# A sliding-window attention and MoE kernel: fewer f32 loads at the start, masks built earlier, and a new hand-written order

## The chip, the core and the metric

The kernel runs on one core of a Trainium2 chip. A core has five engines with queues of their own: TensorE (PE, matrix products into PSUM; its weight loads are the row PEld), VectorE (DVE), ScalarE (ACT), GpSimd (POOL) and SyncE (SP). SP, ACT and POOL also issue DMAs, which sixteen DMA engines carry out. The metric is the device time of one launch in microseconds (us), the median of several runs; lower is better.

## The reference

Two stages. Attention over 8 batches, 8 heads, 576 positions and head size 64; heads 0 to 3 look back over 32 neighbours (plain heads), heads 4 to 7 over 32 positions at a stride of 4 (dilated heads). Its output, 4608 rows of 512, goes through a two-layer network with a SiLU between.

```python
mask_plain = (rel >= 0) & (rel < window)                                   # window = 32
mask_dil = (rel >= 0) & (rel < window * dilation) & (rel % dilation == 0)  # dilation = 4
scores = np.where(masks, scale * q @ k.T, -1e9)
attn = softmax(scores) @ v
...
x = attn_out.transpose(0, 2, 1, 3).reshape(B * S, H * D)   # 4608 x 512
h = x @ w_in                                               # 512 -> 2048
g = h * (1.0 / (1.0 + np.exp(-h)))
return g @ w_out                                           # 2048 -> 512
```

## The kernel before

All work is in f16 with f32 sums. The attention is computed batch by batch, the network in ten groups of tokens: groups 0 and 1 have 256 tokens each, all of batch 0, groups 2 to 9 have 512. A group needs the attention output of the batches that its tokens lie in, so attention of later batches is mixed with the network of earlier tokens.

**Steps and the table.** Every piece of work is a step with a short name, and the long string TABLE (lines 11 to 117) lists the steps in the order in which they are put into the engines' queues. Nothing reorders them afterwards: each engine takes its own instructions in the table's order and waits where data is not there. A name's first token emits its PE part into the PSUM buffers named behind the equals sign (a, b, x, y, u, z, or s for a pair); each later token emits the next part on another engine (A is ACT, D is DVE; S and A behind an output step name the queue that issues its store). The names that matter below:

- `0N0` and so on: early casts and clears of batch 0, without PE work.
- `bTA..`, `bTD..`, `bTS..`, `0TR`: transposes on PE that turn loaded q and k of batches 0, 1 and 2 (`b`) so that the head dimension lies on partitions; TD is for dilated heads.
- `bS0` to `bS6`: scores and their exponential; `bP..` and `bD..`: attention times v for plain and dilated heads; `bXP..`, `bXD..`: transposes of the result into the network's input `xA`.
- `lg.f`: layer 1 of group g, columns f (four matmuls); for groups 8 and 9 `lg.j.i` is one of seven smaller products of a Strassen scheme. `yg.t.n`: layer 2, for groups 2 to 9 again seven products. `u`, `a`, `t`, `w`, `v`: sums for these schemes, on DVE.
- `z..`: a filler matmul on nothing.

**Loads.** The input is f32. Nearly all loads are issued by POOL and cast to f16 on the way (`issue_part`, `issue_vraw`, `issue_vp_first`, then the list ORDER). They come back to back: batch 0, then w_in in the pieces w0b, w0a, w1, w2, w3, then batch 1 (d1, p1), w_out mixed with batch 1's v, then batch 2 (`0B`). Three loads at the very start are uncast and issued by SP: the dilated heads of k and q of batch 0 (`issue_raw`, line 282, 384 KB each, into memory that later holds `kqT`), which the steps 0N0 to 0N3 cast on ACT and DVE, and the head of v (line 336, 96 KB, into `xA`), which 0N12 casts into `vp`.

**Batches 3 to 7** take another way: POOL casts q and k into DRAM (`issue_cast`, line 286, tensor kq_s), and SP reads them back with transposing DMAs (`issue_turn`, lines 300 and 303, steps `bT`, four each: k and q of plain heads into `nat`, k and q of dilated heads into `kqT`). The POOL step `bL` (`loads_gen`) waits for an earlier batch's `kqT` with two tiny copies (line 477), loads v, and issues the cast. For batches 5 to 7 the result goes to DRAM (`bW0` to `bW3`, line 708) and comes back transposed into `xA` (`bX0`, `bX1`, line 469), all on SP. The steps `f0` to `f10` (`hold`, line 1055) are tiny POOL copies that read a finished layer-1 column, so that what stands behind them in POOL's queue comes no earlier; `f2` reads column 3 of group 6, the output of `l6.3`.

**The start in code order.** SP's three loads, clears, eight warm-up matmuls (line 340), the clear of the identity on DVE, POOL's first load (k), the identity on POOL (line 344), POOL's other loads, a clear of `vraws[1]` on ACT (line 351), more clears on DVE, and then the masks (lines 364 to 371), which need the identity.

Of the kernel before, what the change touches and what calls it, by code (L numbers as in the profile page):

```python
# [23 lines left out]
l1.9=t 1TS0=D 1TS0=A 1TS1=a 1TS1=D 1S6=s l1.11=t y0.0.0=y 1TS1=D l1.9 1S6 1S3 0B l1.11 l1.10=t 1S6 l1.8=a
1S4=s 1TA1k=z 1S4 1S4 l1.10 1V1=A 1S5=bx 1S5 y0.1.0=u 1TA1k=D 1S4 1S5 l1.8=t 1S2=s 1S2 1S2 1S0=xz 1V0=D 1D03=b
1D03 1D03 1S0 l1.8 y0.1.1 y0.0.1 1S0 1S6 1S1=s 1S1 1S5 1D10=a 1D02=x 1D02 1D02 1D10 1S0 1D11=z 1D12=b 1D10
y0.0.2 l1.14=x l1.14=s y0.1.2 1D12 1D01=a 1D12 1S2 1D13=b y0.1.3 y0.1.3=A 1D11 1D01 y0.0.3 1S1 1D13 y0.0.3=A
y1.0.0=x 1D01 w1 1D11 1S1 1D00=y 1P3=z 1P0=u 1D13 1P3 1P1=b 1P1 1P3 1P4=a y1.0.1 1D00 l1.13=z l1.13=t 1P4 1D00
1P0 1P0 1XD0=y 1XD0=A 1P1 y1.0.2 1XD0=A l1.13 1P4 1P2=u 1XP3=b 1XP1=y 1XP1=D y1.0.3 y1.0.3=A 1P2 1P2 1XP0=a
2TA1k=z 1XP3=D 1XP4=u 1XP2=y 1XD1=b 1XP4=A 2TD3=x 2TD1=u 1XP0=D 1XP2=A 2TD3=D 1P5=a 1P5 2V0=A 1XD1=A 1XD1=A  # L30
2TD1=A l2.1=y l2.0=x y0.1.3=A 1P5 l2.1=s l2.0=t 2TA1k=D 2TD0=u 2TD2=z y1.1.0=y 2TD0=A 2TD2=D 2S5=s 2S4=ub 2S4
2S4 w1 2S6=za y1.1.1 2S5 y1.1.2 y1.1.3 2S6 2S5 2V1=A w1 l2.0 2S3=s 2S6 w0 y1.1.3=A v1 2TS0=a 2TS0=A 2TA1q=b
2TA1q=A 2TA0q=x 2TS1=z 2TA0k=y 2TA0k=A 2TA0q=D 2TS1=D 2S3 l2.2=u 2TS0=D 2S1=xb l2.2=t 2TS1=D 2S0=ya 2S1 2S3
2S0 2S2=s 2S2 l2.3=z l2.3=t l2.4=x 2S3 2S0 2S1 l2.2 l2.8=u l2.8=s 2S0 l2.6=y l2.4=s l2.6=s 2S4 l2.5=a l2.5=s
l2.3 2S6 2D03=b 2D03 2D03 l2.7=z 2S1 2P1=u 2P1 l2.10=b 2D01=y l2.7=s 2P1 l2.10=s 2D00=u 2D01 2S5 2XP1=x 2XP1=A
l2.9=a 2D01 2D00 2D00 2D12=b 2D10=y 2D12 l2.11=x 2P0=z l2.9=s 2D10 2D10 2D13=a 2D11=u l2.11=s l2.14=y 2D12 2P0
2D13 2D13 2P2=b 2D02=a l2.13=x 2D11 2P0 2P2 2D11 l2.12=u l2.14=s l2.13=s 2D02 2D02 0B 3T 3T 3T 3T 3L 2P2
2XD0=y 2S2 2S2 y1.1.3=A l2.12=s w0 2XP0=z 2P3=a l2.15=x 2XP0=A 3L 2XD0=A 2P3 2P3 y0.0.3=S 2XD0=A u2.0=D 3S2=s
l2.15=s 2XD1=a 2XP2=z u2.0=D 1XP5=u 4L 2XP3=b y2.0.0=y 2XP2=A 1XP5=A 2XP3=A 2XD1=A u2.2=D 2XD1=A u2.2=D l3.0=b
u2.1=D y2.0.0=A u2.0=D v0 l3.1=a l3.0=s u2.2=D 2P5=z l3.3=x l3.1=s 2P5 u2.2=D u2.1=D y2.0.1=u u2.1=D l3.3=t  # L40
u2.0=D y2.0.2 y2.0.1=A 2P5 u2.1=D 2P4=z y1.0.3=A y2.0.3 y2.0.2=D 4L l3.3 y2.0.4 3S2 3S2 y2.0.3 2P4 2P4 4L
3S0=xa w0 3S5=s 3S1=zb 3S0 y2.0.5 y2.0.4 3S5 3S5 3S1 4T y2.0.6 y2.0.5 3S1 3S0 y2.0.5=A 2XP5=x 3S3=s y2.0.6=D
2XP5=A 3S4=zb 3S0 y2.0.6=A l3.4=a 3S4 3S1 3S4 l3.5=y 3S3 3S3 3S4 3P3=u l3.7=x 3P3 3P3 3S2 2XP4=b y2.1.0=u
3V0=D l3.5=s 3S5 l3.6=z l3.4=s 3V1=A 3S3 2XP4=A l3.7=s 3P2=y 3P0=a l3.10=b 3P2 l3.6=t y2.1.0=D 3P2 3P0 y2.1.2
l3.6 l3.10=s 3P0 3D11=x 3D01=y 3P5=b 3D11 l3.14=a 3D01 3D01 3D11 l3.2=z 3P5 l3.14=s 3P5 4T y2.1.2=A 3P1=b
3D03=x l3.2=s y2.1.1=y 3P1 3P1 3D03 3XP0=b l3.13=z y2.1.1=D 3D03 u3.0=P y2.1.3 l3.13=s 3XP0=D 4T l3.9=a y2.1.3
3XP2=x 3D02=z l3.9=s 3D13=b 4T y2.1.5 3D02 3D13 3D02 3XP2=A y2.1.4 y2.1.5 3D13 3XP1=a 3D00=y y2.1.4 3XP3=x
# [12 lines left out]
4XP2=D y3.1.6 5S4 5S4 y3.1.5 4D10=x 5S3 l5.9=y 4D10 u4.2=P y3.1.6=D 4D10 y3.1.6=S 5S2=ab l5.9=t 5S0=s u4.0=D  # L60
y3.1.5=S l5.13=u 5S2 5S4 5S2 l5.5=z 5S3 5S0 5S0 l5.9 l5.6=b u4.0=D y4.0.0=y u4.0=D l5.5=s 5S5 4XP5=x y4.0.1=a
l5.6=s y4.0.0=D 6T 5S1 l5.13=s l5.10=b u4.2=D 4XP5=A u4.2=D u4.2=D u4.1=D l5.2=x l5.10=s u4.1=D y4.0.1=A
4XD1=z y3.0.6=A y4.0.2 4XD1=D l5.2=s u4.1=D 4XD1=A y4.0.3 y4.0.2=D 5D01=x 6T y4.0.4 5D01 5D02=z l5.12=u y4.0.4
5D01 6V1=D l5.8=b 6V0=D 5S2 6T l5.15=x 5D02 l5.8=t 5D02 l5.12=s y4.0.3 l5.11=z l5.8 6T 5S0 y4.0.5 l5.11=s
l5.15=s y4.0.6 y4.0.5 f1 u5.1=D y4.0.5=S 5P1=a 5P5=z y4.0.6=A 5D00=x 5P0=u 5P5 l5.14=b 5P1 y4.0.6=S 5P5 5P0
5P0 l5.4=z 5D00 l5.14=s 5P1 7L u5.2=D 5D11=u 5P4=b l5.4=s l5.0=y 5D11 5D00 5D11 u5.2=D l5.7=a u5.1=D l5.0=t
u5.1=D 5D12=z y4.1.0=u l5.7=s 5P4 l5.0 5P4 l5.3=a y4.1.0=A 5D12 5D12 u5.1=D y4.1.1=x l5.3=s l5.1=z y4.1.1=A
5D10=y 5P3=a l5.1=s 5D03=b 5D10 y4.1.2 5D10 u5.2=D u5.0=D y4.1.3 5P3 5P3 6S2=s y4.1.2=D 6S0=ay 5D03 6S2 6S2
5D13=z 5D03 y4.1.4 y4.1.3 5W2 6S0 5P2=b 6S0 y4.1.5 5P2 5P2 y4.1.4 5W0 6S1=s y4.1.5 6S5=ba 6S1 6S1 y4.1.6 a4=P
y4.1.5=S 5D13 5W1 5D13 6S5 y5.0.0=y u5.0=D y4.1.6=A 6S5 u5.0=D y5.0.1=b y4.1.6=A 5X0 y5.0.0=A u5.0=D y5.0.2  # L70
y5.0.1=A u5.2=D 7V0=A 5W3 6S0 6S3=ax 6S4=s 6S5 6S3 y5.0.3 y5.0.2=A 6S4 6S4 y5.0.4 y5.0.3 6S3 6S4 6P1=z 6P0=a
y5.0.5 y5.0.4 6P0 6P0 l6.3=u 6S3 6P1 6P1 l6.7=x l6.3=s y5.0.5 a0=D l6.14=a f2 7L y5.0.6 l6.14=s l6.7=t 7L
l6.9=z y5.0.6=A l6.7 y5.0.5=A l6.5=y l6.9=s f3 f0 6D02=x l6.15=a l6.5=t 6D02 6D02 y5.0.6=A 6S1 6D00=z 6D11=u
# [49 lines left out]
def kernel(  # L123
# [148 lines left out]
    def issue_part(src, m0, m1, dst, h0, h1):  # L272
        rows = src[0].rearrange("h (m r) d -> m h (r d)", r=DIL)
        nc.gpsimd.dma_start(  # L274
            out=dst[: m1 - m0, h0:h1].rearrange("p h r d -> p h (r d)"), in_=rows[m0:m1, h0:h1]
        )

    raw = [t.bitcast(F32)[:MA, : HN * DIL * D] for t in kqT_flat]

    def issue_raw(i, src):  # L280
        rows = src[0].rearrange("h (m r) d -> m h (r d)", r=DIL)
# [820 lines left out]
```

## Time and profile before

| | us |
|---|---|
| median of 3 runs | 296.58 (296.05 to 297.59) |
| the profiled execution | 296.87 |
| its span, first to last instruction | 295.1 |
| PE busy | 283.3 (96%) |
| DVE busy | 220.9 (75%) |
| ACT busy | 186.3 (63%) |
| POOL busy, DMA issues counted | 55.5 (19%) |

All times below are from the start of that span. The granted PE clock is 1.00 in every stretch, so no time is lost to the clock. PE's busy share is near 100% from 25 us to 290 us, with a few gaps; the text of the prediction shows them. The DMA engines are busy without a break from 2 us to about 55 us and move some 190 to 205 GB/s of written bytes there; from 55 us on there are pauses.

### The profile page before, as it was taken

The numbers are of one execution on the slowest core, as the hardware profiler recorded it, in microseconds if no ns is written. First come the engines' busy times: TensorE is split into PE (matmuls) and PEld (weight loads), VectorE is DVE, ScalarE is ACT, GpSimd is POOL, SyncE is SP. The second block draws the span as 40 slices with busy tenths as digits, with TensorE's granted clock in tenths as the row PEclk, the third lists the DMA queues.
The fourth block names the chain that finished last, engine by engine and source line by source line (L and its number), as shares of the span: only waits on it lengthen the run. The fifth ranks groups of instructions, "written<-read, shape, count | busy, mean of one in ns | idle before, by whom it ended". The sixth has DMA issues, their size and how long they took to land.

```text
span 295.1 us, 7444 instructions
## 1 busy us (share of the span) xinstructions
PE 283.3 (96%) x2976; PEld 201.7 (68%) x2976; DVE 220.9 (75%) x652; ACT 186.3 (63%) x399; POOL 55.5 (19%) x91
## 2 busy tenths in 40 slices
PE   6988999899999999999999999978999999999994
PEld 2667755555586767467666875657557888888884
DVE  7772688668988696476978785785869988968842
ACT  6886873898787477757835765446565376374620
POOL 8854724001540060005002004000000000000000
PEclk9999999999999999999999999999999999999999
DMA  8999999999999989989998249998534002012022
GB/s 167 185 203 196 203 195 190 200 194 181 159 130 218 188 148 174 202 163 120 225 221 176 71 122 101 200 192 192 155 80 117 36 3 107 2 72 73 3 105 108
DMA packets 100107, 42.66 MB, mean 145 GB/s; under 512 B 68584, under 2 KB 95464, under 8 KB 100072
## 3 DMA queue, kind: packets, MB, share of 16 engines
q0 software_dynamic: 47728, 19.47, 54.3%
q1 hardware_dynamic: 50328, 19.04, 30.2%
q10 hardware_dynamic: 2016, 3.67, 3.6%
q8 instruction: 23, 0.38, 0.5%
q14 instruction: 12, 0.10, 0.1%
HBM read 39.81 MB, written 17.10 MB: 193 GB/s over the span
## 4 chain that ended last, share of the span: by engine, by line
PE 77%; DMA 16%; POOL 2%; SPq 1%; issue 1%; ACT 0%; POOLq 0%
PE y L997 32%; PE h L812 28%; PE h L900 8%; DMA nat<-in_q_dram 6%; DMA nat<-in_k_dram 4%; DMA w_in<-in_moe_w_in_dram 3%; PE s L618 3%; DMA w_out<-in_moe_w_out_dram 3%; PE av_d L673 2%; DMA kqT<-kq_s 2%; PE av_p L673 2%; PE y L936 1%; SPq L300 1%; POOL nat L274 1%; PE xd L729 1%
## 5 line engine op out<-in xcount | busy, mean ns | idle before, releaser
L812 PE MATMUL h<-xA,w_in 128*128 128x512 f16 (+1 forms) x512 | 108.0, 352 | 1.9 <-DMA w_in<-in_moe_w_in_dram 1.9
L821 ACT ACTIVATE gT<-h 128x512 f16<-128x512 f32 (+1 forms) x103 | 54.3, 553 | 32.5 <-PE h L812 32.0
L812 PEld LDWEIGHTS <-w_in 128*128 128x128 f16 x512 | 45.8, 97 | 36.5 <-DMA w_in<-in_moe_w_in_dram 2.2
L997 PEld LDWEIGHTS <-gT 128*128 128x128 f16 x512 | 49.0, 98 | 7.2
L997 PE MATMUL y<-w_out,gT 128*128 128x256 f16 x384 | 48.8, 273 | 0.0
L997 PEld LDWEIGHTS <-work 128*128 128x128 f16 x384 | 36.8, 98 | 5.6
L997 PE MATMUL y<-w_sum,work 128*128 128x256 f16 x256 | 32.5, 273 | 0.0
L673 PEld LDWEIGHTS <-probs 128*128 128x128 f16 x448 | 21.8, 97 | 9.9 <-DVE oP L678 0.6
L1023 DVE TENSOR_TENSOR ob<-y,nat 128x256 f32<-128x256 f32 x48 | 19.9, 419 | 10.0 <-PE y L997 8.9
L678 DVE TENSOR_TENSOR oD<-av_d,rcps 72x256 f16<-72x256 f32 x64 | 26.1, 416 | 1.1
L632 ACT ACTIVATE probs<-s 128x384 f16<-128x384 f32 (+2 forms) x48 | 20.5, 483 | 7.1 <-PE s L618 7.0
L627 ACT ACTIVATE probs<-s 128x768 f16<-128x768 f32 (+2 forms) x27 | 20.9, 776 | 3.6 <-PE s L618 3.4
L826 DVE SCALAR_TENSOR_TENSOR gT<-th,h 128x512 f16<-128x512 f32 (+1 forms) x25 | 14.2, 574 | 9.8 <-ACT th L824 9.5
L678 DVE TENSOR_TENSOR oP<-av_p,rcps 96x256 f16<-96x256 f32 x48 | 19.7, 415 | 0.8
L824 ACT ACTIVATE th<-h 128x512 f32<-128x512 f32 (+1 forms) x25 | 12.9, 518 | 11.3 <-PE h L812 11.0
L487 ACT COPY nat<-y 128x256 f32<-128x256 f32 x28 | 10.3, 374 | 15.1 <-PE y L997 11.3
L1055 POOL COPY fence<-gT 128x1 f16<-128x1 f16 x11 | 1.7, 188 | 95.9 <-ACT gT L821 67.4
L676 DVE RECIPROCAL rcps<-av_d 72x4 f32<-72x4 f32 x64 | 10.5, 172 | 11.3 <-PE av_d L673 11.1
L997 PE MATMUL y<-w_sum,gT 128*128 128x256 f16 x128 | 16.6, 273 | 0.0
L997 PE MATMUL y<-w_out,work 128*128 128x256 f16 x128 | 16.6, 273 | 0.0
L936 PE MATMUL y<-w_out,gT 128*128 128x512 f16 x64 | 15.6, 379 | 0.0
L477 POOL COPY fence<-kqT 128x1 f16<-128x1 f16 x10 | 3.5, 353 | 64.5 <-DMA kqT<-kq_s 64.5
(128 smaller groups left out, 462.2 us busy)
## 6 DMA issues: line engine op xcount, KB each, us to landing
out_dram<-ob SPq DMA_DIRECT2D x22, 256.0 KB, 2.7
out_dram<-ob ACTq DMA_DIRECT2D x14, 256.0 KB, 3.2
kq_s<-in_k_dram POOLq DMA_DIRECT2D x5, 576.0 KB, 9.8
kq_s<-in_q_dram POOLq DMA_DIRECT2D x5, 576.0 KB, 13.1
vp<-in_v_dram POOLq DMA_DIRECT2D x7, 384.0 KB, 8.0
w_out<-in_moe_w_out_dram POOLq DMA_DIRECT2D x4, 512.0 KB, 10.5
vraw<-in_v_dram POOLq DMA_DIRECT2D x8, 224.0 KB, 5.4
w_in<-in_moe_w_in_dram POOLq DMA_DIRECT2D x3, 512.0 KB, 11.3
```

Source lines behind the costliest of these rows:

```text
L627: nc.scalar.activation(p2, both[:, :, :n], AF.Exp, scale=scale)
L632: nc.scalar.activation(p2[:, i], sp[i][:, :n], AF.Exp, scale=scale)
L673: nc.tensor.matmul(a[:, i, : D + 1], lhs(i), rhs(i), start=True, stop=True)
L678: nc.vector.tensor_tensor(o, a[:n, :, :D], rcp[:n, :, None].broadcast_to([n, HN, D]), ALU.mult)
L812: nc.tensor.matmul(h[:, :w], w_in16[:, c, f * P : (f + 1) * P], x_g[:, c], start=(c == 0), stop=(c == HP - 1),)
L821: nc.scalar.activation(o, h[:, :w], AF.Silu, scale=2.0)
L824: nc.scalar.activation(th[:, :w], h[:, :w], AF.Tanh)
L826: nc.vector.scalar_tensor_tensor(o, th[:, :w], 1.0, h[:, :w], ALU.add, ALU.mult)
L900: nc.tensor.matmul(y, lhs[:, c, j], rhs[:, c], start=first and c == 0, stop=c == 1, skip_group_check=not first,)
L936: nc.tensor.matmul(y, gTs[g][:, f, tb * P : (tb + 1) * P], w_out16[:, f], start=(f == 0), stop=(f == NFF - 1),)
L997: nc.tensor.matmul(y, lhs[:, c, tb * P : (tb + 1) * P], rhs[:, c], start=first and c == 0, stop=c == KP - 1, skip_group_check=not first,)
L1023: nc.vector.tensor_tensor(half, y, (u2, t5, t1)[n - 3], ALU.add)
```

## The change

Only k of batch 0's dilated heads still comes as f32 over SP. The same heads of q become a cast load on POOL, the first one in its queue, behind the identity. The head of v is cast straight into `vp` by a POOL load in place of SP's load and the step 0N12. Both `vraws` are cleared on ACT. The masks are built on DVE right behind the start, ahead of the other clears. The casts 0N2 and 0N3 of q are gone, so the clears are renumbered 0N2 to 0N9.

```diff
-    raw = [t.bitcast(F32)[:MA, : HN * DIL * D] for t in kqT_flat]
-    def issue_raw(i, src):
-        rows = src[0].rearrange("h (m r) d -> m h (r d)", r=DIL)
-        nc.sync.dma_start(out=raw[i].rearrange("p (h x) -> p h x", h=HN), in_=rows[:MA, HN:])
+    raw = kqT_flat[0].bitcast(F32)[:MA, : HN * DIL * D]
+    v_head = vps[0].rearrange("p (i j) c -> p i j c", i=HN)[:, :, 0, :D]
...
-    v_head = xA[:, HP - 1, : 2 * HN * D].bitcast(F32).rearrange("p (h d) -> p h d", h=HN)
-    issue_raw(0, k)
-    issue_raw(1, q)
-    nc.sync.dma_start(out=v_head[W:], in_=v[0, :HN, :QB].rearrange("h s d -> s h d"))
+    nc.sync.dma_start(
+        out=raw.rearrange("p (h x) -> p h x", h=HN),
+        in_=k[0].rearrange("h (m r) d -> m h (r d)", r=DIL)[:MA, HN:],
+    )
...
     nc.vector.memset(ident_w, 0.0)
-    nc.vector.memset(vraws[0], 0.0)
-    issue_part(k, 0, MA, nat_of(0, "k"), 0, HN)
+    nc.vector.memset(v_head[:W], 0.0)
+    for t in vraws:
+        nc.scalar.copy(
+            t.rearrange("p a h r d -> p (a h r d)").bitcast(F32).rearrange("p (n c) -> p n c", n=4),
+            warm.bitcast(F32)[:, None, :].broadcast_to([P, 4, GT // 2]),
+        )
     nc.gpsimd.affine_select(
         out=ident, in_=ident, compare_op=ALU.not_equal, fill=1.0, base=0,
...
+    issue_part(q, 0, MA, nat_of(0, "q"), HN, H)
+    issue_part(k, 0, MA, nat_of(0, "k"), 0, HN)
     issue_part(q, 0, MA, nat_of(0, "q"), 0, HN)
     issue_vraw(0, (0,))
+    nc.gpsimd.dma_start(out=v_head[W:], in_=v[0, :HN, :QB].rearrange("h s d -> s h d"))
     issue_vp_first(1, 3)
-    nc.scalar.copy(
-        vraws[1].rearrange("p a h r d -> p (a h r d)").bitcast(F32).rearrange("p (n c) -> p n c", n=4),
...
+    nc.vector.tensor_tensor_scan(
+        band, ident, ident_w[:, :P], 0.0, ALU.add, ALU.subtract
     )
-    nc.vector.memset(v_head[:W], 0.0)
+    nc.vector.tensor_scalar(band, band, 1.0, BIG, ALU.subtract, ALU.mult)
+    nc.vector.tensor_copy(mask_d[:, :6], band[:, None, :MH].broadcast_to([P, 6, MH]))
+    nc.vector.tensor_copy(mask_d[:, 6:], band[:, None, P - MH :].broadcast_to([P, 4, MH]))
+    nc.vector.tensor_copy(mask_p, band[:, None, W:].broadcast_to([P, 6, QB]))
+    nc.vector.memset(mask_p[:W, :2], -BIG)
     nc.vector.memset(act_one, 0.0)
...
-    nc.vector.tensor_tensor_scan(
...
-            for n in range(4):
+            for n in range(2):
                 add(("N", n), lambda eng, n=n: cast_raw(eng, n), False)
             for n in range(NP):
-                add(("N", 4 + n), lambda eng, n=n: clear(eng, n), False)
-            add(("N", 4 + NP), lambda eng: v_first(eng), False)
+                add(("N", 2 + n), lambda eng, n=n: clear(eng, n), False)
```

The whole table is new. PE's work is the same but for the fillers, ten in place of six; most steps stand within a few microseconds of PE work of where they stood. The stretches that the prediction speaks of, first the table before, then the new one:

```text
before, where batch 2's transposes begin:
1XP2=y 1XD1=b 1XP4=A 2TD3=x 2TD1=u 1XP0=D 1XP2=A 2TD3=D 1P5=a 1P5 2V0=A 1XD1=A 1XD1=A
2TD1=A l2.1=y l2.0=x y0.1.3=A 1P5 l2.1=s l2.0=t 2TA1k=D 2TD0=u 2TD2=z y1.1.0=y 2TD0=A
after:
0B 3T 2TA1k=a 2TA1k=A 1XP0=b y1.1.0=y 1XP2=A 1XP0=D 1XD1=A 1XD1=A 1P5=b 1P5 1P5 y1.0.3=A
l2.1=z l2.1=s 2TD0=x 2TD1=b 2TD0=A 2TD1=D 2TD2=a 2TD2=D 2TD3=u 2TD3=D

before, the loads and casts of batch 7:
l6.3=u 6S3 6P1 6P1 l6.7=x l6.3=s y5.0.5 a0=D l6.14=a f2 7L y5.0.6 l6.14=s l6.7=t 7L
...
l6.9=z y5.0.6=A l6.7 y5.0.5=A l6.5=y l6.9=s f3 f0 6D02=x l6.15=a
after:
5W0 y4.1.6 y4.1.6=A u5.0=D y4.1.5 6S4 y5.0.0=y y5.0.1=b u5.0=D y5.0.0=A 6P0=x 5W3 7L 6P0
...
5X0 l6.3=u l6.3=s l6.14=z l6.7=a l6.14=s l6.7=s 6S1 5W1 6S3
...
f2
...
6D01 l6.15=s 7L 6D02=b
6D02 6D00=x l6.5=s u6.2=P l6.13=z l6.0=s f1 a0=D 7L
```

The store of `y0.1.3` moves from ACT's queue (issued at 54.15 us before) to SP's, ahead of batch 3's transposing DMAs; the stores of `y1.0.3`, `y0.0.3` and `y1.1.3` are now on SP behind them.

## The prediction

> **What bounds the kernel now.** First the busy shares: PE 96%, DVE 75%, ACT 63%. PE is the bound, so the question is where PE stands still. The view of busy time by stretch (stretch, its length, each engine's busy us and instructions, granted clock, DMA share, GB/s) shows four places:
>
> ```profile
> core 0: us, PE busy (x) PEld busy (x) DVE busy (x) ACT busy (x) POOL busy (x), PEclk, DMA share, GB/s
> 20.00:25.00 5.00, 3.49 (x42) 3.04 (x41) 2.36 (x9) 2.88 (x9) 1.41 (x2) 1.00 1.27 205
> 50.00:55.00 5.00, 4.10 (x58) 2.69 (x56) 2.83 (x11) 2.71 (x8) 0.15 (x1) 1.00 1.80 182
> ...
> 195.00:200.00 5.00, 3.07 (x47) 2.58 (x46) 4.36 (x11) 2.87 (x6) 0.00 (x0) 1.00 1.04 195
> 200.00:205.00 5.00, 4.10 (x64) 3.48 (x63) 1.85 (x5) 3.27 (x9) 0.00 (x0) 1.00 0.83 197
> ```
>
> Then the timeline of PE there (start, us, what, idle time before it and its releaser):
>
> ```profile
> 23.99 1.27 PE L812 MATMUL h<-xA,w_in 128*128 128x256 f16 x10 [0.84 <-DMA w_in<-in_moe_w_in_dram]
> ...
> 53.48 0.63 PE L533 MATMUL td<-ident_w,nat 96*128 96x96 f16 x11 [0.90 <-DMA nat<-in_q_dram]
> ...
> 198.43 0.70 PE L618 MATMUL s<-nat 64*128 64x96 f16 x24 [1.93 <-DMA nat<-kq_s]
> ...
> 202.75 0.70 PE L618 MATMUL s<-kqT 64*128 64x72 f16 x32 [0.90 <-DMA kqT<-kq_s]
> ```
>
> All four wait for a DMA. The chain of waits says the same of the first 53 us: it runs through loads, not through work.
>
> ```profile
> 7.41 8.45 DMA w_in<-in_moe_w_in_dram
> ...
> 16.14 10.72 DMA nat<-in_k_dram
> ...
> 27.14 7.44 DMA w_out<-in_moe_w_out_dram
> ...
> 36.77 16.58 DMA nat<-in_q_dram
> ```
>
> And the timeline of POOL shows what starts batch 7's loads: a fence that waited 17 us for layer 1's output.
>
> ```profile
> 176.68 0.19 POOL L1055 COPY fence<-gT 128x1 f16<-128x1 f16 x1 [17.18 <-ACT gT L821]
> 177.51 1.43 POOL L323 DMA_DIRECT2D vp<-in_v_dram  x1 [0.65 <-issue]
> 178.94 0.79 POOL L286 DMA_DIRECT2D kq_s<-in_k_dram  x1
> ```
>
> **A ruler for the new order.** PE executes the table in order, so I gave every step its own PE time from this trace: 0.86 us for `l` of 512 tokens (four matmuls), 0.44 for 256, 0.87 for `y`, 0.22 for a Strassen product, 0.12 for `P` and `D`, 0.13 to 0.29 for scores and transposes, 0.55 to 0.6 for batch 0's scores with their mask matmuls. Summed along the table this is 270.5 us in both kernels (fillers left out: they lie where PE waits anyway, and end before 17 us of it). The position of a step on this ruler is its work ahead; actual start minus position is the time lost so far. Before, that loss is 11.0 us at `l0.8` (23.99 us, position 12.97), 12.3 at 2TD3, 13.35 behind its wait, 16.54 at `l6.3`, 19.8 behind batch 7's waits, 20.6 at the end: the last 85 us lose 0.8. What can be won lies in these waits, 1.0 + 1.06 + 2.1 + 1.07 us counted by the ruler.
>
> **The change, part by part.**
>
> *The load stream.* Removed from SP: q, 96 x 1024 f32 = 393 KB, and v's head, 98 KB. From 2.5 to 5 us the uncast loads moved 282 GB/s: 393/282 = 1.4 us; v's head shared 5 to 7 us with casts, some 0.45. Added on POOL's queue: q as 197 KB of f16 at the 196 GB/s of the casts from 7 to 8 us = 1.0, and v's head, 49 KB in short rows at 169 GB/s (13.5 to 15.5 us, where such rows run) = 0.3. The stream is 0.5 us shorter. Everything behind on POOL is issued two issues (2 x 0.7 us) later, but the chain shows POOL already issuing ahead of landings from 7.4 us on, so the issues hide behind landings. Bounds: the first cast load before was issued at 1.29 and landed at 7.12, behind SP's loads, though one issued at 158.15 into idle engines landed in 3.5. If half of the freed time or more is lost to a late start of the queue, the stream is 0.6 later; if the cast loads fill SP's gap whole, 0.9 earlier. I take 0.5 earlier, since the first landing before follows the end of SP's traffic.
>
> By the Trainium skill's page "DMA: Bandwidth & Descriptors", section "Where 436 GB/s comes from", a load from HBM is bound by what HBM gives one core, about 358 GB/s; a cast load would then cost its f32 bytes, and this term would be about 0 in place of 0.5. The trace doesn't agree: 196 GB/s written as f16 are 392 GB/s read.
>
> *The start.* ACT keeps two casts (0.62 each, now both of k), DVE loses two (0.88 together), and 0N12 (0.42, ACT) goes. Other copies change sides: ACT's instructions from 4.7 us to the SiLU table load, each at its row's time, add up to 13.1 us against 12.1, so the load, which stood at 17.29, comes near 18.3. The clear of `vraws[0]` (0.91, DVE) becomes 1.04 on ACT at 3.1 us, where it was idle; the masks lie on DVE before 5 us in both. The first transpose waited for q's cast until 6.86; now for q's landing, 5.6 to 8.2 (from 393 KB and 197 KB at the rates above; from 6.5 us to landing, the slowest of line 274's loads, behind an issue at 1.7). None of this shows: `l0.8` waits for w2, which landed at 23.94, and stands at 12.97 in both tables. From `l0.0` at about 18.3 there are 4.2 us of PE work to it, 22.5, against w2 at 23.4. **-0.5**, cover 0.9 us; past that each us of a late start costs one.
>
> *Batch 2's transposes.* 2TD3 stood at position 40.08 and met q's landing at 53.34. Now 2TA1k, needing k alone, goes first, then `y1.1.0` and `l2.1`, and the first TD stands at 41.93. With the loss at `l0.8` now 10.5, plus the 1.27 that small bubbles added on the way, PE gets there at 53.7; q lands at 52.8, or 53.7 if the store of `y0.1.3`, now issued by SP near 46 us into the middle of the stream, takes its 262 KB out of it at 282 GB/s. Either way next to no wait: **-1.06** (0 at worst).
>
> *Batch 7.* From the fence at 176.68, plain scores could start 21.75 us later (198.43) and dilated ones 26.07 (202.75). The fence fires 1.73 us behind the start of `l6.3` (174.95), so they need 23.5 and 27.8 us from there. The ruler had 21.4 us of PE work between `l6.3` and 7S0: wait 2.1. Now `l6.3` stands at 156.54 in place of 158.41 and 7S0 at 180.66 in place of 179.78: 24.1 us, no wait. 7S3, first to need `kqT`, has 26.4 ahead: wait 1.4. Of 3.2 us 1.4 stay: **-1.8** (0 to -3.2). On POOL the cast now stands behind `f1` too, a copy of 0.19 whose column is old. The sums marked P run on DVE as before.
>
> *What comes in.* `l6.3` now follows 1.9 us earlier on batch 5's return, and SP does 5W3 (0.87) ahead of 5X0. 5X0 follows 5W0 by 2.3 (167.47 to 169.79) and lands by 3.3 (median of line 469); 5W0 follows 5P2 (position 150.18) by 1.0. That makes 156.8 against 156.5: **+0.3** (0 to 1.5). Three stores move behind 3T on SP, to some 70 us; their buffers are wanted again at `y2.0.3`, near 81. **+0.2** for small bubbles of another order. 3S0, 4S0, 5S1 and 6S0 stand within 1.1 us of where they stood, and what releases their loads moves with PE.
>
> Sum: 296.87 - 0.5 - 1.06 - 1.8 + 0.3 + 0.2 = 294.0 against the profiled execution, which stands 0.29 over the median: **293.7**.
>
> **Rivals.**
>
> *The stream starts late.* For: line 274's loads took 5.8 to 6.5 us to land at the start. POOL's queue then has q and v's head more and starts as late as before: stream +0.6. `l0.8` at 24.6, loss 11.6; at 2TD 12.9 in place of 13.35, so 0.45 won there; 296.87 - 0.45 - 1.8 + 0.5, less 0.29: 294.8. Against: SP's loads, which held it up, are less than half.
>
> *Batch 7's chain is bound elsewhere.* If 5X0 holds `l6.3` by 1.5 us (DRAM stores have taken 3.6 to land) or the cast finds the DMA engines busy with stores, the third term goes to 0 or into the new wait: 296.87 - 0.5 - 1.06 + 0.5, less 0.29: 295.5 to 296.5, no change or nearly.
>
> *PSUM buffers come round too soon (slower).* In the new table 194 buffers come back to PE within 2.0 us of PE work, 179 before (below 0.8 us 13, 9 before). Each needs a drain, an ACT or DVE copy of 0.3 to 0.6 and the hand-over: about 0.35 too long where the copying engine is an instruction behind. Fifteen such cost 5.2 us: 293.7 + 5.2 = 298.9. It decides once the engines run more than an instruction (0.4 us) late at them, 10 times or more for a loss. Against: before, outside the DMA waits no bubble behind 24 us exceeds 0.2, with 179 such places; and DVE, 9.6 of 10 us busy from 220 to 230, has less in the new order (640 instructions for 650).
>
> **How the numbers follow.** Two runs of one kernel differ by 0.5% (1.5 us) at most, so less is no change. Chances: forecast 0.58, own range 291.8 to 295.0 (-0.9 in the stream, -3.2 at batch 7; the upper ends the other way); late stream 0.14; batch 7 elsewhere 0.12; slower 0.16. Faster by over 0.5%: nearly all of the first two and little of the third, 0.71; within 0.5%: 0.12; slower 0.17. The range takes in the first three up to no change: 291.6 to 297.2.
>
> **What would show it.** Right: the `h` wait for w_in near 23.5; no wait of `td` on `nat` at 53; the fence on `l6.3` near 173; the wait for `nat<-kq_s` gone and one of 1 to 2 us on `kqT<-kq_s` left; PE's total unchanged at 270.5 by the ruler. Wrong: `h` waiting for `xA` at `l6.3`; `l0.8` past 24; many waits of PE on ACT or DVE in the middle. The prediction falls if waits of that last kind sum to 3 us.

## The result and the profile after

| | before | after |
|---|---|---|
| median of 19 runs each, us | 296.83 (295.39 to 300.15) | 295.25 (293.60 to 298.21) |
| the profiled execution, us | 296.87 | 294.57 |
| its span, us | 295.1 | 292.8 |
| PE busy | 96% | 97% |

The ratio of the times is 0.9942, with a 95% interval of 0.9918 to 0.9966: 0.6% faster. The forecast was 293.7, 1.5 us below the median, which lies outside the range given for the forecast alone (291.8 to 295.0) and inside the whole range. Measured once more beside the last experiments, the same kernel had a ratio of 0.9995 (0.9967 to 1.0023). All 31 runs of it have a mean of 295.88 us, all 89 runs of the kernel before 296.97; the difference is 1.1 us, give or take 0.5 (1.96 standard errors). So the gain is real but small, and less than the first comparison says. The prediction took 1.5 us as the most by which two runs of one kernel differ; the 89 runs of the kernel before lie between 294.95 and 300.27.

The busy time by stretch of the kernel after, in the stretches that were shown of before and in one more (the columns are those named in the header):

```profile
core 0: us, PE busy (x) PEld busy (x) DVE busy (x) ACT busy (x) POOL busy (x), PEclk, DMA share, GB/s
20.00:25.00 5.00, 4.75 (x58) 4.04 (x58) 3.04 (x14) 4.17 (x10) 1.25 (x2) 1.00 1.25 206
50.00:55.00 5.00, 5.00 (x56) 2.89 (x55) 2.95 (x12) 2.10 (x7) 0.94 (x2) 1.00 1.44 217
195.00:200.00 5.00, 5.00 (x65) 4.30 (x64) 3.85 (x10) 3.45 (x5) 0.00 (x0) 1.00 1.19 232
200.00:205.00 5.00, 5.00 (x86) 4.36 (x84) 4.62 (x12) 4.98 (x11) 0.00 (x0) 1.00 1.14 168
170.00:175.00 5.00, 4.64 (x53) 3.50 (x52) 3.84 (x10) 4.21 (x9) 0.00 (x0) 1.00 0.59 161
```

The holes at 53 us and at 195 to 205 us are closed. A new one stands at 170 to 175 us, where PE of the kernel before was busy for all 5.00 us. The timeline of PE of the kernel after names the steps:

```profile
20.21 0.30 PE L667 MATMUL av_d<-vd,probs 128*128 128x65 f16 x4 [0.52 <-DVE xA L488]
20.34 1.47 PE L805 MATMUL h<-xA,w_in 128*128 128x256 f16 x12
...
25.03 2.13 PE L805 MATMUL h<-xA,w_in 128*128 128x256 f16 x18
...
55.28 1.24 PE L532 MATMUL td<-ident_w,nat 96*128 96x96 f16 x24
...
174.25 2.10 PE L805 MATMUL h<-xA,w_in 128*128 128x512 f16 x9 [0.35 <-DMA xA<-x_s]
...
198.55 0.69 PE L617 MATMUL s<-nat 64*128 64x96 f16 x24
...
201.03 0.69 PE L617 MATMUL s<-kqT 64*128 64x72 f16 x32
```

Batch 2's TD and batch 7's two scores (the lines at 55, 198 and 201) no longer carry a wait in brackets. But `l0.0` comes at 20.34, before it came at 18.19, and `l0.8` at 25.03 in place of 23.99, and it waits for nothing: w2 had landed at 23.37. `l6.3` now waits for `xA`. The chain of waits of the kernel after (start, us, what) has lost the loads behind the first; up to 53 us it is now made of work:

```profile
1.54 5.10 DMA nat<-in_q_dram
6.69 1.06 PE td L541 x11
20.51 1.31 PE h L805 x12
22.53 1.44 PE h L805 x12
25.20 6.99 PE h L805 x64
```

And the timeline of POOL shows the fence 0.7 us earlier than before (176.68):

```profile
175.97 0.19 POOL L1048 COPY fence<-gT 128x1 f16<-128x1 f16 x1 [16.98 <-ACT gT L814]
176.47 1.43 POOL L320 DMA_DIRECT2D vp<-in_v_dram  x1 [0.31 <-PE h L805]
```

One table carries the rest. It gives the loss of the prediction's ruler (actual start less the PE work ahead) at six steps in order of time, for every profiled execution; where a number grows from one column to the next, PE stood still or ran slowly in between.

| us lost at | l0.8 | 3S2 | 6S0 | l6.3 | l7.14 | last y |
|---|---|---|---|---|---|---|
| before | 11.0 | 13.9 | 16.0 | 16.5 | 19.9 | 20.6 |
| after | 12.1 | 14.3 | 16.3 | 17.7 | 18.3 | 18.4 |
| after_again | 11.1 | 14.7 | 16.7 | 18.3 | 19.1 | 19.1 |
| order_alone | 12.2 | 14.4 | 16.5 | 18.3 | 19.3 | 19.4 |
| code_alone | 11.3 | 15.4 | 17.5 | 18.0 | 22.1 | 22.7 |
| clears_early | 12.2 | 14.6 | 16.7 | 20.2 | 21.8 | 21.9 |
| l63_late | 12.4 | 14.7 | 16.7 | 18.4 | 22.4 | 22.5 |
| fillers | 11.6 | 14.3 | 16.4 | 20.4 | 20.9 | 21.0 |
| start3 | 10.4 | 13.1 | 15.1 | 16.6 | 18.1 | 18.2 |
| store_early | 12.2 | 14.5 | 16.5 | 17.8 | 18.9 | 19.3 |
| before_no_fence | 10.5 | 16.8 | 18.9 | 28.3 | 31.0 | 31.6 |
| fillers_drains | 11.4 | 13.9 | 15.9 | 18.9 | 20.2 | 20.3 |
| start3_store | 10.9 | 14.2 | 16.2 | 17.9 | 19.2 | 19.2 |
| start3_store_p2 | 11.0 | 14.0 | 16.0 | 17.3 | 18.8 | 18.9 |

From `l6.3` to `l7.14` the kernel before loses 3.4 us, the kernel after 0.6: this is the gain. The other kernels with the new table, `l63_late` aside, lose 0.5 to 1.6 us there. In the profiled execution the start gives back 1.0, `l6.3` 0.8.

### The profile page after: what moved, and what is told of

It is laid out like the page before. It is cut to its first block, busy times and chain, and to the rows that moved or that the text cites. A ratio compares the mean times of both kernels' runs of the same rounds, so it can differ in the third digit from the quotient of the medians.

```text
span 292.8 us, 7437 instructions
## 1 busy us (share of the span) xinstructions
PE 285.2 (97%) x2978; PEld 203.3 (69%) x2978; DVE 215.8 (74%) x641; ACT 192.0 (66%) x404; POOL 57.0 (19%) x93
## 4 chain that ended last, share of the span: by engine, by line
PE 92%; DMA 3%; DVE 3%; issue 0%; ACTq 0%; ACT 0%; POOL 0%
PE h L805 34%; PE y L990 32%; PE h L893 8%; PE y L929 5%; PE s L617 3%; PE av_d L667 3%; PE av_p L667 2%; DMA nat<-in_q_dram 2%; DMA xA<-x_s 1%; PE xp L707 1%; PE y_warm L1054 1%; PE xd L723 1%; PE td L532 1%; PE s L605 1%; PE ta_k L566 1%; DVE oP L672 1%
## 5 line engine op out<-in xcount | busy, mean ns | idle before, releaser
L814 ACT ACTIVATE gT<-h 128x512 f16<-128x512 f32 (+1 forms) x110 | 58.3, 553 | 34.5 <-PE h L805 33.6
L667 PEld LDWEIGHTS <-probs 128*128 128x128 f16 x448 | 23.2, 97 | 12.4 <-DVE xA L488 0.6
L1016 DVE TENSOR_TENSOR ob<-y,nat 128x256 f32<-128x256 f32 x48 | 19.9, 420 | 14.8 <-PE y L990 11.5
L626 ACT ACTIVATE probs<-s 128x576 f16<-128x576 f32 (+2 forms) x27 | 20.7, 767 | 5.3 <-PE s L617 4.9
L486 ACT COPY nat<-y 128x256 f32<-128x256 f32 x34 | 12.7, 376 | 17.2 <-PE y L990 13.6
L670 DVE RECIPROCAL rcps<-av_d 72x4 f32<-72x4 f32 x64 | 10.9, 173 | 13.8 <-PE av_d L667 13.4
L670 DVE RECIPROCAL rcps<-av_p 96x4 f32<-96x4 f32 x48 | 8.0, 173 | 13.5 <-PE av_p L667 13.3
L667 PE MATMUL av_d<-vd,probs 128*128 128x65 f16 x256 | 16.3, 193 | 0.5 <-DVE xA L488 0.5
L990 PE MATMUL y<-w_out,work 128*128 128x256 f16 x128 | 16.6, 273 | 0.0
L990 PE MATMUL y<-w_sum,gT 128*128 128x256 f16 x128 | 16.6, 273 | 0.0
## 6 DMA issues: line engine op xcount, KB each, us to landing
kq_s<-in_q_dram POOLq DMA_DIRECT2D x5, 576.0 KB, 12.1
```

What stands on the lines that cost most here:

```text
L486: nc.scalar.copy(dst, src)
L626: nc.scalar.activation(p2, both[:, :, :n], AF.Exp, scale=scale)
L667: nc.tensor.matmul(a[:, i, : D + 1], lhs(i), rhs(i), start=True, stop=True)
L670: nc.vector.reciprocal(rcp[:n], a[:n, :, D : D + 1])
L814: nc.scalar.activation(o, h[:, :w], AF.Silu, scale=2.0)
L990: nc.tensor.matmul(y, lhs[:, c, tb * P : (tb + 1) * P], rhs[:, c], start=first and c == 0, stop=c == KP - 1, skip_group_check=not first,)
```

## The experiments

### Which half of the change does it: the loads or the order

`order_alone` is the new table on the old start code, `code_alone` the new start code on the old table.

```diff
 order_alone, in the new table (the clears 0N2 to 0N9 become 0N4 to 0N11)
-0N0=A 0N1=A 0TD0=b
+0N0=A 0N1=A 0N2=A 0N3=D 0N12=A 0TD0=b
 code_alone, in the old table (the clears 0N4 to 0N11 become 0N2 to 0N9)
-0N2=A
-0N3=D
-0N12=A
```

> The new table on the old start code: q and v's head come as f32 over SyncE, with two q casts (one ACT, one DVE) and the cast of v's head (ACT) put back behind the casts of k; the masks are built where they were before. Theory (the new start is late because of its order: the four drains of the dilated transposes stand on DVE, and four clears stand among ACT's exponentials): l0.0 stays near 20.3 us, l0.8 near 25.0 without a wait for w2, batch 7 waits for nothing, and the time is within 0.3 us of the changed kernel, ratio 0.993 to 0.997. Rival (the start is late because q comes as a cast load and lands at 6.64): l0.0 comes back to 18.2 to 18.8 and l0.8 to 23.9, where w2 lands; ratio 0.989 to 0.992.

> The new start code on the old table (its two q casts and the cast of v's head dropped). Theory (order makes the start late, the load code is sound): first scores no later than 7.8 us, l0.0 near 18.2, l0.8 waits for w2, which lands 0.5 earlier at 23.4; the wait of batch 2's TD stays near 0.9 and those of batch 7 near 2 and 1 us; the time falls by the 0.5 of the stream at most, ratio 0.997 to 1.000. Rival (the cast load of q is what is late): first scores at 8.5 or later, l0.8 at 24.5 or later, ratio above 1.000.

`order_alone`: ratio 0.9965 (0.9934 to 0.9995), `l0.0` at 20.46, `l0.8` at 25.15 with w2 landed at 23.22, no wait of batch 7. As the theory had it, and within the scatter of the kernel after: the order alone gives whatever is gained, and the old loads with it start no earlier. `code_alone`: ratio 1.0097 (1.0056 to 1.0137), above 1.000 as the rival had it. The new loads by themselves cost time. The late first scores (8.69), which the rival named as the sign, do not show why: PE's clock was granted at 0.50 there from 8 to 10 us, and `before_no_fence`, with the old loads and the old table, has its first scores at 8.59. What is left is the load stream. Its timeline of PE shows two waits for w_out, which the kernel before does not have:

```profile
36.58 1.04 PE L927 MATMUL y<-w_out,gT 128*128 128x512 f16 x4 [0.30 <-DMA w_out<-in_moe_w_out_dram]
...
41.14 1.24 PE L927 MATMUL y<-w_out,gT 128*128 128x512 f16 x5 [0.67 <-DMA w_out<-in_moe_w_out_dram]
```

These two pieces of w_out landed at 36.54 and 41.09 in place of 34.59 and 39.05, and q of batch 2 at 54.80 in place of 53.34. In the old order these waits push everything behind them (15.4 against 13.9 in the table at 3S2).

### The start: clears, fillers, drains

In the profile after, ACT stood idle from 5.6 to 10.2 us, then worked without a gap until the SiLU table load at 19.84. So the first theory was ACT's queue, with four clears in it.

```diff
 clears_early
-... 0N2=A 0S4=za ... 0N6=A ... 0N5=A ... 0N4=A
+0N0=A 0N1=A 0N2=A 0N6=A 0N5=A 0N4=A 0TD0=b
```

> The changed kernel with ACT's four clears of batch 0's probabilities moved up to right behind the casts of k, where ACT is idle from 5.6 to 10.2 us. Theory (from 10.2 us ACT's queue sets the start): the SiLU table load moves up from 19.84 by up to the 2.2 us of the clears, l0.0 comes at 18.3 to 18.9, l0.8 waits for w2 at 23.4 to 23.7; batch 2's TD then waits some 0.5 for q, unless q moves too; 293.2 to 294.0 us against the profiled 294.57 of the changed kernel, ratio 0.987 to 0.992. Rival (the late first scores, PE and DVE set the start): the table load moves, but l0.0 stays at 19.8 or later and l0.8 at 24.5 or later; ratio as the changed kernel, 0.993 to 0.996.

The table load came at 19.86, `l0.0` at 20.45, `l0.8` at 25.14; ratio 0.9970 (0.9942 to 0.9998). The theory fell: without its clears ACT just waited for PE. The busy time by stretch of `clears_early` shows why (the number behind POOL's is the granted PE clock):

```profile
6.00:7.00 1.00, 0.00 (x0) 0.00 (x0) 0.00 (x0) 1.00 (x3) 1.00 (x2) 1.00 1.37 184
7.00:8.00 1.00, 0.98 (x12) 0.83 (x13) 0.39 (x2) 0.22 (x1) 0.76 (x2) 0.63 1.43 192
8.00:9.00 1.00, 1.00 (x7) 0.61 (x6) 0.87 (x3) 0.00 (x0) 0.71 (x1) 0.50 1.71 180
9.00:10.00 1.00, 1.00 (x8) 0.26 (x8) 0.07 (x2) 0.00 (x0) 0.68 (x1) 0.50 2.12 162
10.00:11.00 1.00, 1.00 (x18) 0.46 (x18) 0.40 (x1) 0.63 (x1) 0.92 (x3) 0.66 1.63 189
11.00:12.00 1.00, 1.00 (x23) 0.48 (x18) 0.57 (x2) 0.73 (x3) 1.00 (x2) 1.00 1.45 195
```

PE ran nothing from 5.2 to 7.0 us, and then at half clock for (1 - 0.63) / 0.5 + 2 + (1 - 0.66) / 0.5 = 3.4 us. `order_alone`, `code_alone` and `l63_late` sum to 3.4 too. In the kernel after the clock's record reads 1.00 throughout, but its matmuls tell otherwise. Its timeline of PE:

```profile
5.15 0.26 PE L541 MATMUL td<-ident_w,nat 96*128 96x96 f16 x1 [0.37 <-ACT nat L486]
6.69 1.06 PE L541 MATMUL td<-ident_w,nat 96*128 96x96 f16 x11 [1.27 <-DMA nat<-in_q_dram]
...
9.14 0.69 PE L605 MATMUL s<-mask_d,ident_w 128*128 128x288 f16 x2
```

The pair of mask matmuls takes 0.69 us. The kernel before took 0.41 in its profile. But `before_no_fence`, whose start is the same code in the same order, took 0.69 as well. The timelines of PE, `before` first:

```profile
6.86 0.81 PE L542 MATMUL td<-ident_w,nat 96*128 96x96 f16 x15 [1.14 <-ACT nat L487]
...
7.72 0.41 PE L606 MATMUL s<-mask_d,ident_w 128*128 128x288 f16 x2
```

```profile
6.99 1.38 PE L540 MATMUL td<-ident_w,nat 96*128 96x96 f16 x15 [1.27 <-ACT nat L485]
...
8.59 0.69 PE L604 MATMUL s<-mask_d,ident_w 128*128 128x288 f16 x2
```

So the half clock did not come in with the change; the profiled execution of the kernel before escaped it. The Trainium skill's page "TensorE: Matmul & The Clock Gate", section "Part 1: The HAM clock gate (the "warmup" mystery)", has this gate: half rate after an idle window of about 3.4 us, full rate after a busy one, with windows that run freely, so that their phase differs from run to run. The 3.4 us of half rate agree; that PE must stand still for a whole window does not, since the longest standstill here is 2.0 us. The next two kernels put work into PE's gap; `start3` also takes the clears and half of the drains out of the way.

```diff
 fillers
-0N0=A 0N1=A 0TD0=b
+0N0=A 0N1=A z40 z41 z42 z43 0TD0=b
 start3: the same, the clears as in clears_early, and
-0TD2=D
+0TD2=A
-0TD1=D
+0TD1=A
```

> The changed kernel with four more filler matmuls ahead of the first TD step, so that PE has work between the warm-up (4.8 us) and the landing of q's dilated heads (6.6 to 7.2). New theory, since moving the clears did not move l0.0: PE stands still there for 1.3 to 1.8 us, and its clock is then granted at 0.50 for about 3.3 us (8 to 11.5 us in the runs whose record shows it), which costs some 1.6 us of the start. Expected: clock 1.00 and mask matmuls of 0.41 us a pair in place of 0.69 from 8 to 12 us, l0.0 at 18.4 to 19.4, l0.8 at 23.4 to 24.2; ratio 0.988 to 0.993. Rival (the engines' chain, above all the four drains on DVE, sets the start): clock or not, first scores at 8.8 or later and l0.0 past 20.0; ratio 0.993 to 0.996.

> The fillers, and besides the four clears moved up as in the clears run and two of the four drains of the dilated transposes (0TD2, 0TD1) on ACT. Clock theory: the fillers bring nearly all, this adds 0 to 0.5 us over the fillers alone. Chain theory: this is what brings l0.0 to 18.4 or earlier and l0.8 to w2's landing at 23.4 to 23.7, the fillers alone do not. Either way batch 2's TD then meets q's landing near 54.5 and waits 0.3 to 0.9 us, unless the loads move with PE; ratio 0.987 to 0.992.

> The changed kernel with the four fillers and the two drains on ACT, the clears left where they were: tells the drains from the clears. If the drains are the rest of what the start lost: l0.0 at 18.4 to 18.8 and l0.8 at 23.3 to 23.8. If the clears are: l0.0 at 18.8 to 19.2 and l0.8 at 24.2 to 24.7, as with the fillers alone.

The timeline of PE of `fillers`:

```profile
4.58 1.91 PE L1052 MATMUL y_warm<-w_sum 128*128 128x512 f16 x4
6.29 1.05 PE L539 MATMUL td<-ident_w,nat 96*128 96x96 f16 x12
...
7.99 0.41 PE L603 MATMUL s<-mask_d,ident_w 128*128 128x288 f16 x2
```

The first scores come 1.15 us earlier than in the kernel after and at full rate. `l0.0` moves from 20.34 to 19.00 and `l0.8` to 24.59, where it waits for w2 again, which in this execution landed as late as 24.54. With the drains on ACT as well, `l0.8` is at 24.36, right behind w2 at 24.31. In `start3` w2 landed at 23.29 and `l0.8` came at 23.34. So the clock is most of what the start lost; beyond it, the start is bound by w2 again, and drains and clears are not told apart. In the five profiles with these fillers the mask pair takes 0.41 each time. In six with the new table and without them it takes 0.64 to 0.69 five times; in `after_again` it takes 0.41, and there the SiLU table load stands at 18.30, `l0.0` at 18.96 and `l0.8` at 24.02 behind w2 at 23.97. With the old table it takes 0.41 in `before` and 0.68 and 0.69 in `code_alone` and `before_no_fence`. What the new order adds is that the half clock shows: in `before_no_fence` `l0.8` still comes at 23.43, in the five with the new table at 25.0 to 25.3. In total little came of the fillers: ratios 0.9950 (0.9910 to 0.9991) for `fillers` and 0.9948 (0.9919 to 0.9977) for `start3`, no better than the kernel after; `fillers_drains` has one execution, 297.11 us. `start3` was ahead of the kernel after by 1.7 us at `l0.8`, 1.1 at `l6.3` and 0.2 at the end. Its fence was 1.1 us earlier too, but `kqT` was 1.7 later, and 7S3 waited 0.97 us; the section on batch 7 shows how much that chain differs from execution to execution.

### The load stream itself

The fourteen profiles also settle the term on the stream. w2 landed at 23.94, 23.22 and 23.11 with the old loads (before, `order_alone`, `before_no_fence`; mean 23.4) and between 23.29 and 24.56 with the new ones (eleven profiles, mean 24.0). These overlap; later in the stream the difference is plainer: the last load of batch 1's q and k landed between 31.76 and 32.06 with the old loads and between 32.01 and 33.23 with the new ones. The busy time by stretch from 2 to 7 us has the reason, first before, then after:

```profile
2.00:5.00 3.00, 3.00 (x8) 1.06 (x7) 2.84 (x17) 1.40 (x3) 2.92 (x6) 1.00 0.94 249
5.00:7.00 2.00, 0.86 (x7) 0.25 (x6) 1.75 (x7) 1.54 (x4) 2.00 (x4) 1.00 1.37 202
```

```profile
2.00:5.00 3.00, 2.79 (x7) 0.76 (x5) 1.86 (x14) 2.53 (x4) 3.00 (x6) 1.00 0.81 165
5.00:7.00 2.00, 0.57 (x6) 0.42 (x7) 0.00 (x0) 0.62 (x2) 2.00 (x3) 1.00 1.33 164
```

By 5 us the new kernel has written 3 x (249 - 165) = 252 KB less, and its loads are 196 + 49 = 245 KB smaller: nothing is gained. From 5 to 7 us it writes another 2 x (202 - 164) = 76 KB less, 0.4 us at 196 GB/s. The cast loads did not move into the time that SyncE left free.

### Batch 7: the distance from the fence

`l63_late` takes the distance back to 21.4 us; `before_no_fence` is the kernel before without the fence.

```diff
 l63_late
-5X0 l6.3=u l6.3=s l6.14=z l6.7=a ... 6P1=u 6P1 a4=D 6P1 y5.0.4
+5X0 l6.14=z l6.7=a ... 6P1=u 6P1 a4=D 6P1 y5.0.4 l6.3=u l6.3=s
 before_no_fence, in the old table
-f2 7L y5.0.6 l6.14=s l6.7=t 7L
+7L y5.0.6 l6.14=s l6.7=t 7L f2
```

> The changed kernel with l6.3 moved behind l6.15, 6P1 and y5.0.4, so that 21.4 us of PE work lie between it and 7S0, as in the kernel before. Theory (the spacing is the whole reason for batch 7's gain): the waits come back as they were, about 2 us at 7S0 and 1 at 7S3, time 2 to 3 us above the changed kernel, ratio 1.000 to 1.005. Rival (the chain from the fence to the landing is shorter by itself now, 20.06 us in place of 21.75, because the DMA engines are freer): fence 2.7 later, so 7S0 waits 0.7 and 7S3 0.1 to 0.3, time 0.8 to 1.0 above, ratio 0.996 to 0.998.

> The kernel before with one step moved: the fence f2 stands behind batch 7's load of v and its casts in POOL's queue, so these no longer wait for l6.3. Theory (the distance from that fence to 7S0 is the whole of the 3.2 us that batch 7 waited): casts issued by 172 or earlier, no wait of PE at 7S0 or 7S3, 2.5 to 3.3 us off, ratio 0.989 to 0.992. Rival (the fence pays for itself: without it the casts and the load share the DMA engines with 5W, 5X0 and the stores, so l6.3 waits for xA): batch 7's waits go, but l6.3 starts 1 to 4 us later; ratio 0.995 to 1.005.

`l63_late`: ratio 1.0121 (1.0061 to 1.0181). Its timeline of PE, the waits alone:

```profile
200.95 0.70 PE L615 MATMUL s<-nat 64*128 64x96 f16 x24 [1.61 <-DMA nat<-kq_s]
205.19 0.70 PE L615 MATMUL s<-kqT 64*128 64x72 f16 x32 [1.69 <-DMA kqT<-kq_s]
```

Both waits are back and the ruler loses 4.0 us where the kernel after lost 0.6. So the distance is the reason for batch 7's gain. The time is above what the theory and its rival had: without the distance the new order is slower than the old one. The small waits of the rival, that the chain is shorter anyway, did not come. From the issue of v to the landing of `kqT` the chain took 22.65 us in the kernel after, 24.16 in `after_again`, which is the same kernel, and 23.18 here; before, it was 25.2 to the start of 7S3. In the ten profiles with the new table and the new distance it took 22.65 to 25.56. In the five where it took over 25 us 7S3 waits for `kqT` again, 0.66 to 1.08 us; in the other five it does not.

`before_no_fence`: ratio 1.0326 (1.0275 to 1.0377). The waits at 7S0 and 7S3 are gone, as the theory had it, but `l6.3` starts at 186.68. Its timeline of PE and SyncE's queue:

```profile
186.68 5.04 PE L810 MATMUL h<-xA,w_in 128*128 128x512 f16 x12 [8.70 <-DMA xA<-x_s]
```

```profile
172.65 4.11 SPq L467 DMA_TRANSPOSE xA<-x_s  x1
```

The casts were issued at 171.69 and 172.47, just ahead of 5X0. Batch 5's return, which took 4.0 us in the kernel after (170.19 to 174.21), took 14.0. The rival was right, and far too mild with its 1 to 4 us: between 6S0 and `l6.3` 9.4 us are lost, against the 3.2 that the fence costs at batch 7. Behind that wait PE also ran at half clock: the clock was granted at 0.50 up to 191 us, and the twelve matmuls took 5.04 us; before, they took 2.75.

### The wait that came in at l6.3

In `clears_early` and `fillers` `l6.3` was 2.5 and 2.7 us later than in the kernel after. The timeline of DVE, first of `clears_early`, then of the kernel after, at the same step of y4.1:

```profile
167.75 0.42 DVE L1014 TENSOR_TENSOR ob<-y,nat 128x256 f32<-128x256 f32 x1 [2.67 <-DMA out_dram<-ob]
```

```profile
165.52 0.43 DVE L1016 TENSOR_TENSOR ob<-y,nat 128x256 f32<-128x256 f32 x1 [0.76 <-PE y L990]
```

The output buffer that DVE waits for is that of `y3.1.6`. The old table stores it early; the new one has the store in ACT's queue at 162.73, 2.8 us ahead of its next use. It landed in 2.57 us in the kernel after, in 4.58 in `clears_early`, 5.13 in `fillers` and 3.81 in `fillers_drains`. A load may be why: the first part of batch 7's v, which POOL issues ahead of the store (157.66 and 158.29 in the kernel after). In the five profiles where the store took 2.0 to 2.6 us this load had landed, or landed at most 0.7 us behind the store's issue; in the three where it took 3.8 to 5.1 us the load landed 3.1 to 4.5 us behind it. No run moves one without the other, so the cause stays open. Behind DVE stand the drains of batch 5, so 5W2, 5W0, 5X0, `l6.3`, and the fence.

```diff
 store_early
-y3.1.6=D 5S4 u4.0=D l5.9=t 5S2 5S0 u4.0=D ... y4.1.2 y3.1.6=A
+y3.1.6=D 5S4 u4.0=D l5.9=t 5S2 5S0 y3.1.6=A u4.0=D ... y4.1.2
```

> The changed kernel with the store of y3.1.6 issued right behind its last copy (table position of y3.1.6=D, near 137 us) in place of 162.7. Theory (what scatters the changed kernel by 2 to 3 us is this store: its buffer is wanted again 2.8 us later, at y4.1, and the store takes 2.6 to 4.6 to land; a late one holds DVE, so 5W2, 5W0 and 5X0, so l6.3, so batch 7's fence): DVE waits for no store there, 5W2 is issued by 166.5, l6.3 starts by 174.5, batch 7 waits under 0.5; times scatter less (highest less lowest under 3 us) and the median falls by 0.3 to 0.8, ratio 0.990 to 0.994. Rival (the scatter comes from elsewhere, 5X0's own landing or the start): same scatter, ratio 0.993 to 0.997.

Ratio 0.9939 (0.9910 to 0.9969), times from 293.67 to 297.10. 5W2 was issued at 166.46 and `l6.3` started at 174.35, as expected, but the scatter of 3.4 us and the median (294.94) are not told from those of the kernel after. The limit of 3 us for the scatter was missed, and `store_early` was profiled once, so it does not show by itself that the store was the cause. That the late store goes with a loss of 2.1 us (`clears_early`) and 2.6 us (`fillers`) between 6S0 and `l6.3`, against the kernel after, is in the table; how much of the scatter it makes is not shown.

### All of it together

`start3_store` joins `start3` and `store_early`; `start3_store_p2` moves 5P2 up as well.

```diff
 start3_store_p2, besides
-y4.1.3 6S0 y4.1.4 5D03 5P2=b 5D13 5D13 6S2=s y4.1.4 6S0 y4.1.5 5P2 5P2 5W2
+y4.1.3 6S0 5D03 5P2=b y4.1.4 5D13 5D13 5P2 5P2 6S2=s y4.1.4 6S0 y4.1.5 5W2
```

> The changed kernel with the start mended (four fillers, four clears moved up, two drains on ACT) and the store of y3.1.6 moved up, so that both places where it lost against the forecast are covered. Theory (these two are what it lost): l0.8 waits for w2 at 23.3 to 23.7, no wait of DVE for a store at y4.1, l6.3 by 173.5; batch 7 waits up to 1.3 us for kqT, since l6.3 now comes earlier and the chain behind the fence is no shorter; 293.8 to 294.8 us median, ratio 0.986 to 0.992, and lower than the changed kernel's beside it. Rival (what the start wins is paid back whole at batch 7): ratio 0.993 to 0.996, as the changed kernel beside it.

> As start3_store, and 5P2 one y step earlier with its DVE work ahead of y4.1.4's, so that 5W0 and with it 5X0 can be issued earlier. If 5X0's release by 5W0's landing is what l6.3 waits for (0.5 to 0.6 us in three profiles): 5X0 issued 0.4 to 0.6 earlier, l6.3's wait below 0.2, median 0.2 to 0.6 below start3_store. Rival (SyncE still issues the other stores first, or batch 7's wait grows by the same): no change against start3_store.

> The changed kernel as it is, beside the two above on one chip. Expected: ratio 0.993 to 0.996; l0.0 near 20.4 and l0.8 near 25.1 as before; l6.3 anywhere from 174.2 to 177, by how long the store of y3.1.6 takes.

Ratios 0.9954 (0.9928 to 0.9981), 0.9954 (0.9938 to 0.9970) and 0.9995 (0.9967 to 1.0023); medians 295.77, 295.62 and 296.20. Both mended kernels are faster than the kernel before; that they beat the kernel after isn't shown, since the intervals overlap, and the first measurement of that kernel was as good. Of the theory's conditions, `l0.8` came at 23.92 and 24.00 (w2 at 23.8), and batch 7 waits 0.66 and 0.96 us for `kqT`; but `l6.3` of `start3_store` came at 174.47, not by 173.5, and the median is 1 us above the 293.8 to 294.8 that were named. The rival's ratio is the one that was measured. In `start3_store_p2` 5X0 went out at 169.45, 0.6 earlier, and `l6.3` had no wait left, but 5P2 itself then waited 0.50 us for a copy on DVE: no gain, as its rival had it. `after_again` met neither its ratio nor its start, since its PE ran at full clock.

## Why the prediction was right and wrong

**What bounds the kernel**: right for three of the four places. Four DMA waits of PE were named; batch 2's and batch 7's are gone, and the one at the start gave way, in the profiled execution, to PE's own slow clock. Of the signs of being right, the fence came at 175.97, not near 173, and no wait was left on `kqT`; two signs of being wrong came, `l0.8` past 24 and `h` waiting for `xA` at `l6.3`.

**Batch 7, -1.8**: the mechanism was right, shown by undoing it in `l63_late`; the size was off. `l6.3` to `l7.14` lost 3.4 us before, 0.6 and 0.7 in the two profiles after: -2.7 to -2.8; over the ten profiles of the new order it is -1.8 to -2.9. The 1.4 us that were to stay at 7S3 went too, since the chain behind the fence was 2.6 us shorter than the one measured before. That was luck: in five of ten profiles of the new order the chain took over 25 us and 0.66 to 1.08 us of that wait were there.

**Batch 2, -1.06**: the wait was gone in the profiled execution, but that only made up for what the start had lost. In `after_again` q landed at 55.61 and TD waited 0.96 us for it, the "0 at worst" of the prediction.

**The load stream, -0.5**: wrong, and the first of the two steps that failed: "The stream is 0.5 us shorter", with "0.5 earlier" taken since the first landing follows the end of SP's traffic. It came 0.5 us later on the mean of the profiles, three of the old loads and eleven of the new. The rival named for this, "the stream starts late", with +0.6 and 294.8, is what happened to the stream, for the reason its bound gave: the freed time was not used. Its `l0.8` at 24.6 came even later in the profiled execution, 25.03, by the clock and not by the stream. The profiled execution alone, with w2 at 23.37, would have hidden this.

**The start**: the second step that failed: "None of this shows: l0.8 waits for w2", with a cover of 0.9 us. The sum over ACT's instructions gave the SiLU table load at 18.3, and at full PE clock it stood there (18.30 in `after_again`). But in five of the six profiles with the new table and no filler in PE's gap PE then ran at half clock: table load at 19.84 to 20.15, `l0.8` at 25.0 to 25.3, cover gone. The clock had been read as "1.00 in every stretch", with no question what keeps it there, and the cover of 0.9 us had no term for it. In place of -0.5 the profiled execution lost 1.0. PE stood still longer there than before (1.6 to 2.5 us, before 1.14), but whether that is the reason stays open, since `before_no_fence` fell to half clock after 1.27.

**l6.3, +0.3 (0 to 1.5)**: too small, though inside its range: 0.8 and 1.1 us in the two profiles after, and outside it with 3.0 and 3.5 where the store of `y3.1.6` was late (`clears_early`, `fillers`). The price list of moved stores had three names; this fourth one, in the middle, was overlooked.

**Small bubbles, +0.2**: in the profiled execution, from 2TD to 6S0 the loss grew by 0.34 more than before. **The last 85 us** lost 0.3 where they had lost 0.8, which no term had.

**The rivals**: PSUM buffers that come round too soon did not show; no new waits of that kind in the middle. The sum of the profiled execution: +1.04 start, -1.05 batch 2, +0.34, +0.84 `l6.3`, -2.83 batch 7, -0.55 end, together -2.2 us on PE.

## What to carry to other kernels

A new order of work can be judged by distances: from what releases a load to who needs it, from a store to the next use of its buffer. Count both kinds, since a step moved ahead shortens one and lengthens the other, and a fence that looks like a loss may be what keeps a short transfer quick. And a gain at one wait counts only as far as the next one: of the 1.7 us that `start3` won at the start, 0.6 were gone at `l6.3` and 0.9 more behind batch 7. One profile of a kernel is one execution: between the two profiles of the kernel after, one and the same program, `l0.8` differs by 1.0 us and the chain of batch 7 by 1.5, as much as the whole gain of 1.1.

## What the hardware showed that had not been expected

- PE standing still for 1.27 us (`before_no_fence`) to 2.5 us (`l63_late`) at the start, between 4.4 and 7.3 us, was enough for half clock, which lasted 3.4 us in the four profiles whose record shows it. The length alone does not decide: 1.34 and 1.49 us in `start3_store_p2` and `start3_store` and 1.8 us in `after_again` left the clock alone.
- The record of the granted clock can miss this: it read 1.00 in the kernel after, in `store_early` and in `before_no_fence`, whose mask matmuls took 0.69 us a pair.
- A transposing DMA that takes 4.0 us took 14.0 with one load and two casts into DRAM issued ahead of it.
- A store of 256 KB issued at the same point of the order landed in 2.57 us in the kernel after and in 5.13 in `fillers`, where a load issued ahead of it had not landed yet.
